# Windowed attention and an ELU feed-forward layer on one core: V held stationary, row sums by a matmul of ones, and every engine's order from a list plan

## The chip, the cores and the metric

The kernel runs on one core of a Trainium2 chip. The metric is the device time of one execution in microseconds (us). Times of single instructions come from one profiled execution; the engines are named as in the profile: PE (matrix engine; PEld its weight loads), DVE (vector engine), ACT (scalar engine), POOL (GpSimd) and SP (which here only issues DMAs).

## The reference

```python
def _attn_ref(q, k, v):                 # q, k, v: (8, 8, 576, 64) float32
    ...
    scores = scale * np.matmul(q, k.transpose(0, 1, 3, 2))
    mask = np.abs(pos[:, None] - pos[None, :]) <= 32
    scores = np.where(mask, scores, -1000000000.0)
    scores = scores - np.max(scores, axis=-1, keepdims=True)
    attn = np.exp(scores)
    attn = attn / (np.sum(attn, axis=-1, keepdims=True) + 1e-09)
    return np.matmul(attn, v)

# x = heads side by side: (4608, 512)
def _moe_ref(x, w_in, w_out):           # w_in (512, 2048), w_out (2048, 512)
    h = x @ w_in
    g = np.where(h > 0.0, h, np.exp(np.minimum(h, 0.0)) - 1.0)
    return g @ w_out
```

## The kernel before

The 4608 tokens (8 batches of 576) are cut into blocks of 64 queries, nine to a batch; a block needs the 128 keys around it. Two blocks make a **pair** (36 pairs of 128 tokens), four pairs make a **tile** of 512 tokens for the feed-forward part (9 tiles).

Per batch: `load_qk` (SP's queue) brings q and k, half the heads at a time, into five staging buffers; `cast` makes bf16 of them (POOL; DVE and ACT for batch 0); `T` turns them on PE, two heads at a time (six small transposes into the one PSUM buffer `psT`, then a copy by ACT, L131, into `qT` or `kT`; its output is scattered: neighbouring elements read land 12 bytes apart). `load_v` (POOL's queue) brings V as bf16 into `vw`, `shift_v` (SP's queue) copies it 64 rows on for the odd blocks. `vw` has 65 columns for each head: the last one holds ones.

Per pair: `QK` writes 16 score matmuls, keys on the partitions, into `psS`; `SM` is one exp on ACT over 128x1024; `MK` multiplies by the window's mask on DVE, two instructions; `AV(i, g)` takes four heads: the probabilities are the weights, V with its column of ones is streamed, 65 columns, so that `o` holds 128 tokens on the partitions and each head's 64 values and row sum beside them. DVE takes the reciprocal of the four sums (L181, 128x4) and multiplies (L183). `X` turns the pair's 128x512 result on PE (four transposes into `psT`), and DVE copies it into `xt` (L197), where the 512 features are on the partitions.

Per tile: sixteen `Hm(t, fo)`, four matmuls of 512 columns each into one of three `psH` buffers, then ACT's exp (`e`, L210) and in `Hv` two DVE instructions (`f`, L216, and `g`, L217). Sixteen steps of `Y(t, s)`, four matmuls of 512 columns each, make the four 128-row outputs of the tile; each is copied by ACT (L232) out of the one `psY` buffer and stored. H of tile t stands between Y of tile t-1.

The order on all engines is that of the program's text. Six steps of pairs come first, with the loads, casts and transposes of batches 1 and 2 at fixed steps; from then on the rest of the attention is dealt out evenly among the slots of H and Y:

```python
                want = base + (goal - base) * (n + 1) // max(1, len(slots) - 2)
                while pos < min(want, goal):
                    rest[pos][1]()
                    pos += 1
```

Of the kernel before, what the change touches and what calls it, by code (L numbers as in the profile page):

```python
# [8 lines left out]
FP32 = mybir.dt.float32  # L9
# [6 lines left out]
def _bap(ap, new_ap):  # L16
    return bass.AP(tensor=ap.tensor, offset=ap.offset,
                   ap=[list(x) for x in new_ap])


@with_exitstack
def kernel(
# [24 lines left out]
    TT = 512  # L47
    NT = N_TOK // TT
    NC = TT // 128
    NFO = D_FF // 128  # L50
    NDO = DM // 128
    VW = D + 1
# [5 lines left out]
    xsp = ctx.enter_context(tc.tile_pool(name="xsp", bufs=3))  # L58
# [11 lines left out]
    ident = const.tile([128, 128], BF16)  # L70
    masks = const.tile([128, 3, QB], BF16)
# [4 lines left out]
    NPB = 2  # L76
# [5 lines left out]
    stage = {}  # L82

    def load_qk(b, half, eng):
        for nm, src in (("q", q), ("k", k)):
            t = stg.tile([PR, HP, TPP * D], FP32, tag="stg")
            eng.dma_start(
                out=t, in_=src[b, half * HP:(half + 1) * HP].rearrange(
                    "h (p t) d -> p h (t d)", t=TPP))
            stage[nm, b, half] = t  # L90

    def cast(b, nm, engs):
        t = bfp.tile([PR, TPP, H, D], BF16, tag="bf")
        for half in range(2):
            src = stage.pop((nm, b, half)).rearrange(
                "p h (t d) -> p h t d", t=TPP)
            dst = t[:, :, half * HP:(half + 1) * HP, :].rearrange(
                "p t h d -> p h t d")
            e = engs[half]
            if e is nc.scalar:  # L100
                nc.scalar.copy(dst, src)
            else:
                e.tensor_copy(dst, src)  # L103
        stage[nm, b] = t

    def load_v(b):
        vt = vw[b % NVB]
        vb = v[b].rearrange("h s d -> s h d")
        nc.gpsimd.dma_start(out=vt[WIN:128, 0, :, 0:D], in_=vb[0:128 - WIN])
        for qb in range(2, NQB - 1, 2):  # L110
            lo = qb * QB - WIN
            nc.gpsimd.dma_start(out=vt[:, qb, :, 0:D], in_=vb[lo:lo + 128])  # L112
        lo = (NQB - 1) * QB - WIN
        nc.gpsimd.dma_start(out=vt[0:S - lo, NQB - 1, :, 0:D], in_=vb[lo:S])
# [6 lines left out]
    def T(b, nm, hp):  # L121
        src = stage[nm, b]
        pt = psT_p.tile([128, TPP, PR], BF16, tag="psT")
        for j in range(TPP):
            nc.tensor.transpose(pt[:, j, :], src[:, j, 2 * hp:2 * hp + 2, :],  # L125
                                ident[0:PR, 0:PR])
        if nm == "k":
            dst = kT[b % NKB][:, hp, WIN:WIN + S]
        else:
            dst = qT[b % NKB][:, hp, :]  # L130
        nc.scalar.copy(dst.rearrange("c (p t) -> c t p", t=TPP), pt)  # L131

    live = {}

    def QK(i):
        psS = psS_p.tile([128, 2, 2, HP, QB], FP32, tag="psS")
# [13 lines left out]
    def SM(i):  # L150
        psS = live.pop(("S", i))
        pu = pup.tile([128, 2, 2, HP, QB], BF16, tag="pu")
        nc.scalar.activation(pu, psS, AX.Exp, scale=SCALE)  # L153
        live["U", i] = pu

    def MK(i):
        pu = live.pop(("U", i))
        p = pm[i % NPB]
        for s in range(2):
            qb = (2 * i + s) % NQB  # L160
            m = masks[:, 1 if qb == 0 else 2 if qb == NQB - 1 else 0, :]
            mb = _bap(m, [m.ap[0], [0, 2], [0, HP], m.ap[1]])
            dst = p[:, :, s * 2 * QB:s * 2 * QB + QB].rearrange(
                "p (a two) c -> p two a c", two=2)
            nc.vector.tensor_mul(dst, pu[:, :, s], mb)  # L165

    def AV(i, g):
        p = pm[i % NPB]
        if g == 0:
            live["X", i] = xsp.tile([128, H, D], BF16, name="xs", tag="xs")  # L170
        o = psO_p.tile([128, HP, VW], FP32, tag="psO")
        for j in range(HP):
            h = g * HP + j
            for s in range(2):
                b, qb = divmod(2 * i + s, NQB)
                nc.tensor.matmul(  # L176
                    o[:, j, :], lhsT=p[:, h, s * QB:s * QB + 128],
                    rhs=vw[b % NVB][:, qb, h, :],
                    start=(s == 0), stop=(s == 1))
        rc = xsp.tile([128, HP], FP32, tag="rc")  # L180
        nc.vector.reciprocal(rc, o[:, :, D])  # L181
        rb = _bap(rc, [rc.ap[0], rc.ap[1], [0, D]])
        nc.vector.tensor_mul(live["X", i][:, g * HP:(g + 1) * HP, :],  # L183
                             o[:, :, 0:D], rb)
# [3 lines left out]
    def X(i):  # L188
        xs = live.pop(("X", i)).rearrange("p h d -> p (h d)")
        t, c = divmod(i, NC)  # L190
        if c == 0:
            xts[t] = xtp.tile([128, NDO, TT], BF16, name="xt", tag="xt")
        pt = psT_p.tile([128, NDO, 128], BF16, tag="psT")
        for do in range(NDO):
# [188 lines left out]
```

## Time and profile before

| | |
|---|---|
| median of 3 runs | 456.05 us (454.32 to 460.13) |
| the profiled execution | 451.61 us, of which the profile's span is 449.9 us |
| mean granted PE clock | 0.981 |
| busy: PE, DVE, ACT, POOL | 337.4, 261.9, 268.3, 84.9 us |
| first matmul of H(0), first of Y(0), last of H(8) | 78.4, 113.2, 427.6 us |

In a line of groups of the profile stand the source line, the engine, the operation, output and inputs with their shapes, the count, the busy time in us and the mean ns of one, then the engine's idle time just before these instructions and what ended it. A row of a single line's view gives the shortest, middle and longest duration in ns. A row of stretches gives each engine's busy us with its instructions in brackets. In a row of the timeline stand the start in us, the length in us, the engine and line, and the idle time before it with its releaser.

### The profile page before, as it was taken

How to read it: one execution, taken by the hardware profiler on the slowest of the kernel's cores; microseconds unless marked ns; L12 is line 12 of the kernel's file. 1: busy time of each engine (PE TensorE's matmuls, PEld its weight loads, DVE VectorE, ACT ScalarE, POOL GpSimd, SP SyncE). 2: the span in 40 equal slices, each digit the busy share in tenths (PEclk: the TensorE clock that was granted, in tenths of full speed). 3: DMA queues.
4: the chain of work that ended last, by engine and by line, in shares of the span. 5: the costliest groups of instructions: out<-in, count | busy, mean ns of one | idle time of the engine just before them, and what ended most of it. 6: DMA issues, size and time to landing. Idle time of an engine off the chain costs nothing.

```text
span 449.9 us, 7032 instructions
## 1 busy us (share of the span) xinstructions
PE 337.4 (75%) x2784; PEld 173.8 (39%) x2832; DVE 261.9 (58%) x557; ACT 268.3 (60%) x283; POOL 84.9 (19%) x92
## 2 busy tenths in 40 slices
PE   0122453766879788788879789687997899999985
PEld 0012342333434344344434345343443444444432
DVE  5004232688746867656757667755666677776610
ACT  1776854788758378637965478476775444344421
POOL 9326216611001700440005200500000000000000
PEclk9999999999989999969999999999899999999999
DMA  8999999973008921972029814520000010010111
GB/s 188 182 261 248 131 216 223 121 80 23 1 23 207 143 50 48 250 60 51 32 66 220 88 32 116 142 72 25 23 25 24 25 48 25 23 48 24 47 48 70
DMA packets 64096, 41.94 MB, mean 93 GB/s; under 512 B 38976, under 2 KB 59456, under 8 KB 64064
## 3 DMA queue, kind: packets, MB, share of 16 engines
q0 software_dynamic: 41728, 8.92, 30.0%
q1 hardware_dynamic: 22336, 32.58, 28.3%
q8 instruction: 22, 0.36, 0.4%
q14 instruction: 10, 0.08, 0.1%
HBM read 36.70 MB, written 9.44 MB: 103 GB/s over the span
## 4 chain that ended last, share of the span: by engine, by line
PE 49%; DVE 17%; ACT 13%; DMA 13%; issue 6%; POOL 1%; SPq 0%; ACTq 0%; POOLq 0%
PE ps L206 20%; PE psY L227 20%; DMA vw<-in_v_dram 6%; DVE g L217 6%; ACT kT L131 5%; DVE f L216 5%; DVE pm L165 5%; DMA w_out_sb<-in_moe_w_out_dram 5%; ACT e L210 5%; PE o L176 4%; DMA t<-in_q_dram 2%; PE pt L125 2%; PE pt L195 2%; ACT qT L131 2%; ACT pu L153 1%
## 5 line engine op out<-in xcount | busy, mean ns | idle before, releaser
L210 ACT ACTIVATE e<-ps 128x512 f32<-128x512 f32 x144 | 92.1, 640 | 113.4 <-PE ps L206 105.6
L206 PE MATMUL ps<-xt,w_in_sb 128*128 128x512 bf16 x549 | 148.6, 389 | 2.8 <-DVE xt L197 1.3
L227 PE MATMUL psY<-w_out_sb,g 128*128 128x512 bf16 x555 | 144.7, 382 | 5.6 <-ACT y L232 3.6
L216 DVE TENSOR_SCALAR f<-e 128x512 bf16<-128x512 f32 x144 | 71.3, 495 | 78.2 <-ACT e L210 78.0
L217 DVE TENSOR_TENSOR g<-ps,f 128x512 bf16<-128x512 f32 x144 | 99.6, 692 | 5.4
L227 PEld LDWEIGHTS <-g 128*128 128x128 bf16 x576 | 52.8, 99 | 58.8 <-issue 6.7
L131 ACT COPY kT<-pt 128x576 bf16<-128x576 bf16 x32 | 66.7, 2084 | 12.0 <-PE pt L125 11.5
L206 PEld LDWEIGHTS <-w_in_sb 128*128 128x128 bf16 x576 | 51.4, 99 | 49.8 <-issue 5.2
L131 ACT COPY qT<-pt 128x576 bf16<-128x576 bf16 x32 | 66.6, 2082 | 5.0 <-PE pt L125 4.7
L125 PE MATMUL pt<-ident,t 96*128 96x96 bf16 x384 | 32.0, 229 | 48.9 <-ACT qT L131 25.4
L176 PE MATMUL o<-vw,pm 128*128 128x65 bf16 x576 | 38.5, 204 | 38.2 <-DVE pm L165 33.5
L103 POOL CAST t<-t 96x1536 bf16<-96x1536 f32 x28 | 41.8, 1522 | 130.8 <-DMA t<-in_q_dram 130.6
L176 PEld LDWEIGHTS <-pm 128*128 128x128 bf16 x576 | 28.6, 104 | 63.3 <-DVE pm L165 54.9
L165 DVE TENSOR_TENSOR pm<-pu,masks 128x512 bf16<-128x512 bf16 x72 | 34.7, 523 | 29.0 <-ACT pu L153 29.0
L125 PEld LDWEIGHTS <-t 96*128 96x128 bf16 x384 | 26.9, 110 | 63.6 <-issue 35.3
L153 ACT ACTIVATE pu<-psS 128x1024 bf16<-128x1024 f32 x36 | 37.2, 1033 | 11.1 <-PE psS L141 8.6
L181 DVE RECIPROCAL rc<-o 128x4 f32<-128x4 f32 x72 | 13.0, 180 | 40.2 <-PE o L176 40.1
L232 ACT COPY y<-psY 128x512 f32<-128x512 f32 x36 | 21.4, 593 | 25.2 <-PE psY L227 24.8
L183 DVE TENSOR_TENSOR xs<-o,rc 128x256 bf16<-128x256 f32 x72 | 30.5, 424 | 2.5
L112 POOL DMA_DIRECT2D vw<-in_v_dram x24 | 21.8, 911 | 25.4 <-PE o L176 13.3
L195 PE MATMUL pt<-ident,xs 128*128 128x128 bf16 x144 | 14.7, 228 | 11.2 <-ACT kT L131 11.1
L197 DVE COPY xt<-pt 128x512 bf16<-128x512 bf16 x36 | 15.0, 417 | 8.6 <-PE pt L195 8.6
(28 smaller groups left out, 72.4 us busy)
## 6 DMA issues: line engine op xcount, KB each, us to landing
t<-in_q_dram SPq DMA_DIRECT2D x16, 576.0 KB, 8.8
t<-in_k_dram SPq DMA_DIRECT2D x16, 576.0 KB, 10.5
out_dram<-y SPq DMA_DIRECT2D x36, 256.0 KB, 2.0
vw<-vw SPq DMA_DIRECT2D x16, 260.0 KB, 5.4
vw<-in_v_dram POOLq DMA_DIRECT2D x24, 128.0 KB, 8.0
w_in_sb<-in_moe_w_in_dram POOLq DMA_DIRECT2D x4, 512.0 KB, 15.6
w_out_sb<-in_moe_w_out_dram POOLq DMA_DIRECT2D x4, 512.0 KB, 25.5
vw<-in_v_dram POOLq DMA_DIRECT2D x16, 96.0 KB, 7.4
```

The costliest lines, as they stand in the source:

```text
L103: e.tensor_copy(dst, src)
L125: nc.tensor.transpose(pt[:, j, :], src[:, j, 2 * hp:2 * hp + 2, :], ident[0:PR, 0:PR])
L131: nc.scalar.copy(dst.rearrange("c (p t) -> c t p", t=TPP), pt)
L153: nc.scalar.activation(pu, psS, AX.Exp, scale=SCALE)
L165: nc.vector.tensor_mul(dst, pu[:, :, s], mb)
L176: nc.tensor.matmul(o[:, j, :], lhsT=p[:, h, s * QB:s * QB + 128], rhs=vw[b % NVB][:, qb, h, :], start=(s == 0), stop=(s == 1))
L183: nc.vector.tensor_mul(live["X", i][:, g * HP:(g + 1) * HP, :], o[:, :, 0:D], rb)
L206: nc.tensor.matmul(ps, lhsT=w_in_sb[:, do, fo * 128:(fo + 1) * 128], rhs=xts[t][:, do, :], start=(do == 0), stop=(do == NDO - 1))
L210: nc.scalar.activation(e, ps, AX.Exp)
L216: nc.vector.tensor_scalar(f, e, -1.0, 0.0, ALU.add, ALU.min)
L217: nc.vector.tensor_tensor(gs[t][:, fo, :], ps, f, ALU.max)
L227: nc.tensor.matmul(ps, lhsT=gs[t][:, fo, c * 128:(c + 1) * 128], rhs=w_out_sb[:, fo, :], start=(fo == 0), stop=(fo == NFO - 1))
```

## The change

**Attention.** `AV(i, s)` now takes one block of 64 queries. For each of the eight heads V (64 columns) is the weight and the head's 64 columns of probabilities are streamed; even heads write PSUM partitions 0 to 63, odd ones 64 to 127, so x comes out with features on the partitions. Two more matmuls with a 128x64 tile of ones as weights and 256 columns streamed give the row sums, each repeated on 64 partitions. `RN` takes the reciprocal of 128x256 sums on DVE and multiplies straight into `xt`. `X`, its transposes and its copy are gone, and so is the column of ones in `vw`.

**Evacuation of q and k.** `E` (ACT, for the last pair of k heads DVE) reads PSUM in steps of 96 elements and writes 576 neighbouring elements. Batch 0's transposes also use the three `psH` buffers. `MK` is one instruction of 128x1024 where both blocks have the same mask.

**Order.** Every operation is entered in a `Plan` with an engine, a duration, a rank and what it needs; `run` then deals them out by time and rank, and calls them in that order.

```diff
+    def run(self):
...
+            for e, rs in ready.items():
+                if not rs:
+                    continue
+                t = max(free[e], min(rs.values()))
+                n = min((ops[n][2], n) for n, r in rs.items() if r <= t)[1]
+                if best is None or t < best[0]:
+                    best = (t, e, n)
...
+        for _, n in order:
+            ops[n][4]()
...
-    vw = [const.tile([128, NQB, H, VW], BF16, name=f"vw{i}") for i in range(NVB)]
-    pm = [const.tile([128, H, 3 * QB], BF16, name=f"pm{i}") for i in range(NPB)]
...
+    vw = [const.tile([128, NQB, H, D], BF16, name=f"vw{i}") for i in range(NVB)]
...
+        if b == 0 and n % 4:
+            pt = psH_p.tile([128, TPP, PR], BF16, name="psH", tag="psH")
+        else:
+            pt = psT_p.tile([128, TPP, PR], BF16, name="psT", tag="psT")
...
-        nc.scalar.copy(dst.rearrange("c (p t) -> c t p", t=TPP), pt)
...
+        dst = dst.rearrange("c (p t) -> c p t", t=TPP)
+        src = pt.rearrange("c t p -> c p t")
+        if EVAC[nm, hp] == "ACT":
+            nc.scalar.copy(dst, src)
+        else:
+            nc.vector.tensor_copy(dst, src)
...
-    def AV(i, g):
...
-                nc.tensor.matmul(
-                    o[:, j, :], lhsT=p[:, h, s * QB:s * QB + 128],
-                    rhs=vw[b % NVB][:, qb, h, :],
-                    start=(s == 0), stop=(s == 1))
-        rc = xsp.tile([128, HP], FP32, tag="rc")
-        nc.vector.reciprocal(rc, o[:, :, D])
...
+    def AV(i, s):
+        p = live["P", i]
+        b, qb = divmod(2 * i + s, NQB)
+        vt = vw[b % NVB]
+        o = psO_p.tile([128, 2, HP, QB], FP32, name="psO", tag="psO")
+        for e in range(2):
+            nc.tensor.matmul(o[64 * e:64 * e + 64, 1], lhsT=ones,
+                             rhs=p[:, e, s], start=True, stop=True)
+        for hp in range(HP):
+            for e in range(2):
+                nc.tensor.matmul(o[64 * e:64 * e + 64, 0, hp, :],
+                                 lhsT=vt[:, qb, 2 * hp + e, :],
+                                 rhs=p[:, e, s, hp, :], start=True, stop=True)
...
+    def RN(i, s):
...
+        rc = rcp.tile([128, HP, QB], FP32, name="rc", tag="rc")
+        nc.vector.reciprocal(rc, o[:, 1])
+        lo = c * 128 + s * QB
+        nc.vector.tensor_mul(xts[t][:, :, lo:lo + QB], o[:, 0], rc)
...
-        pt = psT_p.tile([128, NDO, 128], BF16, tag="psT")
-        for do in range(NDO):
-            nc.tensor.transpose(pt[:, do, :], xs[:, do * 128:(do + 1) * 128],
-                                ident)
-        nc.vector.tensor_copy(xts[t][:, :, c * 128:(c + 1) * 128], pt)
...
+            P.op(("RN", i, s), "DVE", 0.8, r + 1 + s, deps,
+                 lambda i=i, s=s: RN(i, s))
```

What the plan makes of the order is seen at three places. On DVE, in the middle of the run, one pair's work among that of the feed-forward part stood thus before (`pm`: MK; `rc` and `xs`: the two halves of AV; `xt`: X; `f` and `g`: Hv):

```order
L165 TENSOR_TENSOR pm_109<-pu,masks 128x2x4x64 x2
L181 RECIPROCAL rc<-o 128x4
L183 TENSOR_TENSOR xs<-o,rc 128x256
L216 TENSOR_SCALAR f<-e 128x512
L217 TENSOR_TENSOR g<-ps,f 128x512
L181 RECIPROCAL rc<-o 128x4
L183 TENSOR_TENSOR xs<-o,rc 128x256
L216 TENSOR_SCALAR f<-e 128x512
L217 TENSOR_TENSOR g<-ps,f 128x512
L197 COPY xt<-pt 128x4x128
```

and stands now (`rc` and `xt`: RN of the two blocks):

```order
L238 TENSOR_TENSOR pm<-pu,masks 128x1024
L298 TENSOR_SCALAR f<-e 128x512
L303 TENSOR_TENSOR g<-psH,f 128x512
L271 RECIPROCAL rc<-psO 128x256
L273 TENSOR_TENSOR xt<-psO,rc 128x4x64
L298 TENSOR_SCALAR f<-e 128x512
L303 TENSOR_TENSOR g<-psH,f 128x512
L271 RECIPROCAL rc<-psO 128x256
L273 TENSOR_TENSOR xt<-psO,rc 128x4x64
L298 TENSOR_SCALAR f<-e 128x512
L303 TENSOR_TENSOR g<-psH,f 128x512
```

The copy into `xt` is gone, the reciprocal has 64 times the elements, and a pair of `f` and `g` stands between any two steps of the attention.

On POOL, behind batch 0's V and at the start of the program, stood the weights, then batch 1 (`vw_106`) and its casts:

```order
L276 DMA w_in_sb<-in_moe_w_in_dram 128x4x512 x4
L280 DMA w_out_sb<-in_moe_w_out_dram 128x4x512 x4
L109 DMA vw_106<-in_v_dram 96x8x64
L112 DMA vw_106<-in_v_dram 128x8x64 x3
L114 DMA vw_106<-in_v_dram 96x8x64
L103 CAST t<-t 96x4x6x64 x4
```

Now batch 2's V (here `vw_108`) and a cast of batch 0 come first, and between `w_in` and `w_out` stand nine casts and batch 1's V (here `vw_107`):

```order
L195 DMA vw_108<-in_v_dram 96x8x64
L198 DMA vw_108<-in_v_dram 128x8x64 x3
L200 DMA vw_108<-in_v_dram 96x8x64
L164 CAST bf<-stg 96x4x6x64
L341 DMA w_in_sb<-in_moe_w_in_dram 128x4x512 x4
L164 CAST bf<-stg 96x4x6x64 x4
L195 DMA vw_107<-in_v_dram 96x8x64
L198 DMA vw_107<-in_v_dram 128x8x64 x3
L200 DMA vw_107<-in_v_dram 96x8x64
L164 CAST bf<-stg 96x4x6x64 x5
L346 DMA w_out_sb<-in_moe_w_out_dram 128x4x512 x4
```

So `w_out` is issued behind the first cast of batch 3, which takes a buffer that batch 1's transposes must have left.

On SP, batch 1's `shift_v` stood behind eight loads of q and k (`t`; those of batch 0 stand ahead of these rows):

```order
L118 DMA vw_105<-vw_105 64x4x520
L119 DMA vw_105<-vw_105 64x4x520
L87 DMA t<-in_q_dram 96x4x384
L87 DMA t<-in_k_dram 96x4x384
L87 DMA t<-in_q_dram 96x4x384
L87 DMA t<-in_k_dram 96x4x384
L118 DMA vw_106<-vw_106 64x4x520
L119 DMA vw_106<-vw_106 64x4x520
```

Now eighteen loads stand ahead of it, those of batch 3 and the first two of batch 4 among them, and each from the sixth on takes one of the five staging buffers that a cast must have left:

```order
L149 DMA stg<-in_k_dram 96x4x384 x2
L149 DMA stg<-in_q_dram 96x4x384 x4
L204 DMA vw_106<-vw_106 64x4x512
L205 DMA vw_106<-vw_106 64x4x512
L149 DMA stg<-in_q_dram 96x4x384
L149 DMA stg<-in_k_dram 96x4x384 x3
L204 DMA vw_108<-vw_108 64x4x512
L205 DMA vw_108<-vw_108 64x4x512
L149 DMA stg<-in_k_dram 96x4x384 x2
L149 DMA stg<-in_q_dram 96x4x384 x5
L149 DMA stg<-in_k_dram 96x4x384
L204 DMA vw_107<-vw_107 64x4x512
```

The shift of batch 2 (`vw_108`) is issued ahead of that of batch 1 (`vw_107`).

More of the change, by code (lines that the diff above doesn't have):

```diff
@@ L70 @@
     ident = const.tile([128, 128], BF16)
+    ones = const.tile([128, D], BF16)
     masks = const.tile([128, 3, QB], BF16)
@@ L119, in shift_v @@
         nc.sync.dma_start(out=vt[QB:128, 1:NQB:2], in_=vt[0:QB, 2:NQB:2])
[L121 to L133, printed above, removed]
     def QK(i):
-        psS = psS_p.tile([128, 2, 2, HP, QB], FP32, tag="psS")
+        psS = psS_p.tile([128, 2, 2, HP, QB], FP32, name="psS", tag="psS")
         for s in range(2):
@@ new lines, with WI @@
+    sizes = [4] * 9
+    tiles, where = [], {}
+    p0 = 0
+    for t, n in enumerate(sizes):
+        for c in range(n):
+            where[p0 + c] = (t, c)
+        tiles.append((p0, n))
+        p0 += n
+    NT = len(tiles)
+    P = Plan()
+    FC = 512
+    NWC = D_FF // FC
+    w_in_v = moe_w_in.rearrange("(o p) f -> p o f", p=128)
+    w_out_v = moe_w_out.rearrange("(o p) f -> p o f", p=128)
+    def WI(c):
+        nc.gpsimd.dma_start(out=w_in_sb[:, :, c * FC:(c + 1) * FC],
+                            in_=w_in_v[:, :, c * FC:(c + 1) * FC])
@@ L317 @@
[L317 to L352 removed]
+        P.run()
```

411 lines of the change are left out of this document (261 added, 150 removed).

## The prediction

> **What bounds the kernel now.** I read the page from the top: the span, the engines' shares, the slices, the chain; then stretches of the run.
>
> ```profile
> span 449.9 us, 7032 instructions
> PE 337.4 (75%) x2784; PEld 173.8 (39%) x2832; DVE 261.9 (58%) x557; ACT 268.3 (60%) x283; POOL 84.9 (19%) x92
> PE   0122453766879788788879789687997899999985
> DMA  8999999973008921972029814520000010010111
> PE 49%; DVE 17%; ACT 13%; DMA 13%; issue 6%; POOL 1%; SPq 0%; ACTq 0%; POOLq 0%
> 0.00:78.40 78.40, 22.42 (x300) 17.98 (x301) 22.24 (x51) 46.72 (x27) 36.19 (x51) 1.00 1.54 207
> 118.40:401.00 282.60, 243.93 (x2002) 122.03 (x2037) 189.63 (x406) 174.39 (x199) 36.97 (x31) 0.97 0.35 73
> 401.00:449.90 48.90, 42.07 (x189) 18.64 (x191) 19.02 (x34) 14.83 (x25) 0.00 (x0) 1.00 0.13 49
> ```
>
> The last three rows are stretches: length, then busy us of PE, PEld, DVE, ACT and POOL, the granted clock, the DMA share (1 is one full set) and GB/s. There are three regimes. Until 78.4 us PE works 22 us and the DMA slices read 8 or 9: the kernel fills. From 118 to 401 PE is busy 244 of 283 us, and DVE only 190 of 283 (67%). The last 49 us are feed-forward work alone. What PE waits for in the middle, and how the first stretch ends:
>
> ```profile
> PEld L176 <- DVE pm L165: 54.9, 66, 3.4
> PE pt L125 <- ACT qT L131: 25.4, 11, 9.9
> 74.52 0.66 PE L125 MATMUL pt<-ident,t 96*128 96x96 bf16 x6 [4.70 <-POOL t L103]
> 78.44 0.59 PE L206 MATMUL ps<-xt,w_in_sb 128*128 128x512 bf16 x1 [0.51 <-DVE xt L197]
> 113.19 1.03 PE L227 MATMUL psY<-w_out_sb,g 128*128 128x512 bf16 x4
> ```
>
> These are a wait's total us, count and longest, and rows of the timeline. In order, PE stands behind masks and q/k evacuations. H(0) starts at 78.4 because a transpose of batch 2 stands in front of it and waits for a cast. Y(0), and with it H(1), starts at about 112. The end:
>
> ```profile
> L206 PE MATMUL ps<-xt,w_in_sb x549: 377/379/634, 78.4 to 427.6; 128*128 128x512 bf16 x183
> 401.03 1.03 PE L206 MATMUL ps<-xt,w_in_sb 128*128 128x512 bf16 x4
> 401.90 1.03 PE L227 MATMUL psY<-w_out_sb,g 128*128 128x512 bf16 x4
> ```
>
> Four matmuls of 512 columns follow the last four after 0.86 us. H(8) ends at 427.6, so with its sixteen H and sixteen Y in turn (27.5 us) it starts at about 400. From H(1) to there it is 288 us, **41 a tile**.
>
> **What the change does to PE.** H and Y stay as they are. The attention's steps in rows without a wait inside them:
>
> ```profile
> 360.57 0.41 PE L141 MATMUL psS<-qT,kT 64*128 64x64 bf16 x16
> 357.42 0.41 PE L176 MATMUL o<-vw,pm 128*128 128x65 bf16 x8
> 359.39 0.39 PE L195 MATMUL pt<-ident,xs 128*128 128x128 bf16 x4
> 115.36 0.42 PE L125 MATMUL pt<-ident,t 96*128 96x96 bf16 x6
> ```
>
> A pair loses 2 x 0.41 (AV) and 0.39 (X), 1.21 us. It gains twice eight 64-column matmuls and two of 256 columns a block. The eight cost between half of L141's row (0.2, two at a time) and L176's row (0.41); the two cost between 0.11 and 0.22 (half of a 512-column matmul each, together or one after the other). So AV is 0.31 to 0.63 a block; I take 0.5, near the upper row, since its weights change at each matmul as in L176. A pair saves between -0.05 and 0.59 us, 36 pairs between -2 and 21. That shows only if PE remains the bound.
>
> **What it does to DVE: the term that decides.**
>
> ```profile
> L217 DVE TENSOR_TENSOR g<-ps,f 128x512 bf16<-128x512 f32 x144 | 99.6, 692 | 5.4
> L183 DVE TENSOR_TENSOR xs<-o,rc 128x256 bf16<-128x256 f32 x72 | 30.5, 424 | 2.5
> L181 DVE RECIPROCAL rc<-o 128x4 f32<-128x4 f32 x72 | 13.0, 180 | 40.2 <-PE o L176 40.1
> L197 DVE COPY xt<-pt 128x512 bf16<-128x512 bf16 x36 | 15.0, 417 | 8.6 <-PE pt L195 8.6
> L216 DVE TENSOR_SCALAR f<-e 128x512 bf16<-128x512 f32 x144 | 71.3, 495 | 78.2 <-ACT e L210 78.0
> L216 DVE TENSOR_SCALAR f<-e x144: 415/427/1702, 81.0 to 428.6; 128x512 bf16<-128x512 f32 x144
> L165 DVE TENSOR_TENSOR pm<-pu,masks x72: 411/416/5236, 39.1 to 391.9; 128x512 bf16<-128x512 bf16 x72
> ```
>
> From L183 and L217, both with a PSUM input, an element costs (692 - 424)/256 = 1.05 ns and an instruction 424 - 268 = 156 ns. A reciprocal of 4 elements should then take 160 ns; it takes 180. Put on its elements, that is (180 - 156)/4 = **6.0 ns each**. No row shows a long reciprocal, so I bound 128x256 from both sides: 0.42 us if it runs like L183 (the 20 ns being a start-up cost); 2.2 us with the smallest fixed cost that a PSUM row allows, L197's if that copy passes two bf16 at a time (417 - 512 x 0.525 = 148 ns, so 8.0 ns each and 256 x 8.0 + 148). I take 256 x 6.0 + 156 = 1.69 us, the middle, because it is the nearest row of the same operation.
>
> [...]
>
> One RN is then 1.69 + 0.42 + two gaps, 2.2 us. MK becomes one instruction, 0.7 us (between 0.42 and 2 x 0.42). A pair costs DVE 0.7 + 2 x 2.2 = **5.1 us**. The unchanged f and g are 0.43 + 0.69 + gaps 0.06 = 1.18 us for each fo, 18.9 a tile. So a tile takes 4 x 5.1 + 18.9 + 0.6 for one evacuation = 40 us of DVE, against PE's 27.5 (128 matmuls) + 4 x 1.4 + 2.4 = 35.5. DVE becomes the bound at nearly the 41 us that a tile takes now.
>
> **What it does to ACT.**
>
> ```profile
> L131 ACT COPY kT<-pt 128x576 bf16<-128x576 bf16 x32 | 66.7, 2084 | 12.0 <-PE pt L125 11.5
> L210 ACT ACTIVATE e<-ps 128x512 f32<-128x512 f32 x144 | 92.1, 640 | 113.4 <-PE ps L206 105.6
> L153 ACT ACTIVATE pu<-psS 128x1024 bf16<-128x1024 f32 x36 | 37.2, 1033 | 11.1 <-PE psS L141 8.6
> ```
>
> Per element L210 to L153 cost (1033 - 640)/512 = 0.77 ns; 576 neighbouring elements would be 0.69 us, and L131's scattered output takes three times that. Now the output is dense and the PSUM input is scattered. I take 0.7; the upper bound is 2.08 (the scatter costs the same on either side). At 0.7 ACT saves 133 - 39 = 94 us, nearly all beside other work; at 2.08 nothing is saved and the start grows by 10 to 20 us.
>
> [...]
>
> **The start.**
>
> ```profile
> 14.48 1.47 ACT L101 CAST t<-t 96x1536 bf16<-96x1536 f32 x1 [1.56 <-DMA t<-in_k_dram]
> 15.26 0.74 POOL L276 DMA_DIRECT2D w_in_sb<-in_moe_w_in_dram x1 [4.07 <-DMA vw<-in_v_dram]
> 18.07 0.70 SPq L118 DMA_DIRECT2D vw<-vw  x1
> 37.52 0.45 PE L141 MATMUL psS<-qT,kT 64*128 64x64 bf16 x10 [1.88 <-ACT kT L131]
> vw<-vw SPq DMA_DIRECT2D x16, 260.0 KB, 5.4
> t<-in_q_dram SPq DMA_DIRECT2D x16, 576.0 KB, 8.8
> vw<-in_v_dram POOLq DMA_DIRECT2D x24, 128.0 KB, 8.0
> w_in_sb<-in_moe_w_in_dram POOLq DMA_DIRECT2D x4, 512.0 KB, 15.6
> ```
>
> Batch 0's inputs are there at 14.5, its scores at 37.5, behind eight evacuations through one buffer; with four buffers and short copies they start at about 20, and the first AV at 23, when the shift (issued 18.1, 5.4 to land) is there. Four pairs of 2 x (AV 0.5 + handovers 0.2 + RN 2.2) end at 46, where H(0) starts, against 78.4; it takes DVE 19 us, to 65. Then batch 1's shift is missing. SP issues it behind eighteen loads of 576 KB, 10.6 MB; with three batches of V (1.8), two shifts (1.0) and w_in (2.1) that is 15.5 MB, with w_out 17.6. At the 207 GB/s of the first stretch these are 75 to 85 us. On POOL w_out stands behind a cast that waits for batch 1's transposes, at about 60, inside that. So pair 4's second block runs at 80. H(1), Y(0) and the later pairs are queued behind it on PE, and DVE idles from 65. On SP the next loads and the first outputs stand behind the shift; three output buffers cover those. Seven blocks at 2.9 plus 2 for masks make H(1) start at **102** instead of 112. The new tile of ones and the fewer memsets lie under the first loads and cost nothing.
>
> **The sum.** From 102 on DVE has 28 pairs x 5.1 = 143, seven tiles x 18.9 = 132, five evacuations 3 and 7 for waits on POOL's casts (L216's mean, 495 by 71.3/144, is above its middle value): 285 us. Between two RNs stands a pair of f and g, during which PE makes the next AV, so I add only 3%: 294. H(8) starts at 396, the tail stays 49: span 445, and with the 1.7 us around it 447 against 451.6. The median of the runs lies 4.4 us above that execution; added here, **450 us**. The range of this case is 435 to 465.
>
> **The rivals.**
> - *The reciprocal streams* (0.42 us). RN is 0.9, a pair 2.5 us, a tile 29 us of DVE: PE stays the bound. H(1) comes at 80 + 11 = 91; seven tiles at 35.5 with the same 3% are 256, the tail 49: span 396, as a median **402**. For it: 20 ns can be a start-up cost; against it: no other DVE row has one above 160.
> - *The reciprocal takes 8 ns an element* (2.2 us). A pair takes 6.1 us. H(1) comes at 107, then 28 x 6.1 + 142 = 313, with 3% 322; with the tail 478, as a median **485**, slower. It decides from 6.8 ns on, since each ns more is 256 x 72 = 18 us. For it: L197's fixed cost; against it: L183's.
> - *The plan's order does not shorten the start, or E stays at 2.08*: H(1) at 112 or later and the rest as forecast, **455 to 470**. For it: eighteen loads ahead of the shift; against it: the loads are needed later in any case.
>
> **Chances.** Forecast 0.40, streaming 0.27, 8 ns 0.19, the last 0.14. A measurement here tells about 2% (447 to 465) from no change. Of the forecast a third falls below 447, a tenth above 465; streaming is all faster; 8 ns nearly all slower; the last mostly no change. Faster 0.43, same 0.33, slower 0.24. The range of 8 in 10 must reach both reciprocal cases: 388 to 488.
>
> **What would show it.** RECIPROCAL's mean ns at 128x256 settles the main term: 0.4, 1.7 or 2.3 us. DVE should be busy over 85% after 102 us, with PE waiting for RN; with a streaming reciprocal PE is above 93% and DVE near 75%. The copies of q and k should read 0.7 us; H(0) should start at 46 and H(1) near 102, behind batch 1's shift. The forecast is wrong if the reciprocal's cost is not per element, or if in-order waits between PE and DVE cost more than the 3%.

## The result: 439.7 us against 457.4, and the profile after

The changed kernel takes 439.66 us (median of four runs, 438.13 to 440.82) against 457.38 (454.32 to 460.13) of the kernel before, run beside it: a ratio of 0.961, with a 95% interval of 0.954 to 0.969. It is faster by 3.9%, three times the 1.3% that was forecast. The profiled execution took 438.1 us with a span of 436.4.

The page of the changed kernel: span, engines, the granted clock in 40 slices (tenths), the chain that ended last by engine, then the groups of the reciprocal and of a q copy.

```profile
span 436.4 us, 6922 instructions
PE 333.8 (76%) x2786; PEld 166.6 (38%) x2832; DVE 346.6 (79%) x501; ACT 175.2 (40%) x274; POOL 86.4 (20%) x93
PEclk9999999555797999999999999999999999999999
DVE 58%; PE 31%; ACT 5%; DMA 3%; issue 2%; POOL 1%; ACTq 0%; POOLq 0%
L271 DVE RECIPROCAL rc<-psO 128x256 f32<-128x256 f32 x72 | 126.0, 1750 | 16.4 <-PE psO L257 15.7
L187 ACT COPY qT<-psT 128x576 bf16<-128x576 bf16 x30 | 19.1, 636 | 7.6 <-PE psT L174 7.3
```

The chain has gone over from PE (49% before) to DVE (58%). The reciprocal takes 1750 ns where 1.69 us was forecast, the copies 0.64 us where 0.7 was. So the two prices on which the forecast hung were right, and its time was wrong by 10 us nevertheless; where, the stretches show. From here on each kernel is cut at the first `e` of tiles 0, 1 and 8 (1 to 2 us behind that tile's first H). Columns: length, busy us of PE, PEld, DVE, ACT and POOL, clock, DMA share, GB/s. Of the changed kernel:

```profile
0.00:56.30 56.30, 14.43 (x202) 10.85 (x204) 25.34 (x35) 11.56 (x15) 31.46 (x43) 1.00 1.30 239
56.30:119.10 62.80, 41.42 (x435) 24.86 (x438) 44.58 (x61) 29.35 (x44) 20.92 (x20) 0.70 0.86 141
119.10:388.65 269.55, 236.99 (x1968) 112.74 (x2004) 258.57 (x374) 120.05 (x193) 33.98 (x30) 0.99 0.31 64
```

Of the kernel before, the middle:

```profile
113.40:402.10 288.70, 248.76 (x2046) 124.38 (x2084) 194.56 (x417) 179.10 (x205) 36.97 (x31) 0.97 0.34 72
```

Tile 0 starts 24 us earlier than before (56.3 against 80.3), tile 1 **6 us later** (119.1 against 113.4): what the start won is lost again ahead of tile 1. The seven tiles between take 270 us instead of 289, and there DVE is busy 259 of 270 us, 96%. The tail is as it was, 47.8 us. Why tile 1 is late, from the timeline of PE (start, duration, and in brackets the idle time and what ended it):

```profile
83.67 0.66 PE L174 MATMUL psT<-ident,bf 96*128 96x96 bf16 x6
85.06 0.64 PE L174 MATMUL psT<-ident,bf 96*128 96x96 bf16 x6 [0.72 <-ACT qT L187]
...
96.09 0.64 PE L174 MATMUL psT<-ident,bf 96*128 96x96 bf16 x6 [0.73 <-ACT qT L187]
96.66 0.42 PE L253 MATMUL psO<-pm,ones 128*64 128x256 bf16 x2
```

Ten transposes of later batches, about one every 1.4 us because each waits for the copy of the one ahead out of the single buffer `psT`, stand on PE in front of pair 4's second AV at 96.66.

### The profile page after: what moved, and what is told of

Same layout as the page of the kernel before. It is cut to its first block, busy times and chain, and to the rows that moved or that the text cites. A ratio compares the mean times of both kernels' runs of the same rounds, so it can differ in the third digit from the quotient of the medians.

```text
span 436.4 us, 6922 instructions
## 1 busy us (share of the span) xinstructions
PE 333.8 (76%) x2786; PEld 166.6 (38%) x2832; DVE 346.6 (79%) x501; ACT 175.2 (40%) x274; POOL 86.4 (20%) x93
## 4 chain that ended last, share of the span: by engine, by line
DVE 58%; PE 31%; ACT 5%; DMA 3%; issue 2%; POOL 1%; ACTq 0%; POOLq 0%
DVE rc L271 24%; DVE g L303 14%; PE psY L310 12%; PE psH L284 11%; DVE f L298 9%; DVE xt L273 6%; DMA vw<-in_v_dram 3%; PE psT L174 2%; PE psO L253 2%; DVE pm L244 2%; DVE pm L238 2%; PE psS L214 1%; ACT e L292 1%; ACT pu L225 1%; PE psO L257 1%
## 5 line engine op out<-in xcount | busy, mean ns | idle before, releaser
L292 ACT ACTIVATE e<-psH 128x512 f32<-128x512 f32 x144 | 85.9, 597 | 183.5 <-PE psH L284 170.9
L284 PE MATMUL psH<-xt,w_in_sb 128*128 128x512 bf16 x560 | 147.1, 385 | 12.1 <-DVE g L303 7.6
L271 DVE RECIPROCAL rc<-psO 128x256 f32<-128x256 f32 x72 | 126.0, 1750 | 16.4 <-PE psO L257 15.7
L303 DVE TENSOR_TENSOR g<-psH,f 128x512 bf16<-128x512 f32 x144 | 99.6, 692 | 4.9
L164 POOL CAST bf<-stg 96x1536 bf16<-96x1536 f32 x29 | 43.2, 1520 | 100.8 <-PE psT L174 79.3
L253 PE MATMUL psO<-pm,ones 128*64 128x256 bf16 x144 | 23.6, 324 | 46.3 <-DVE xt L273 44.7
L174 PEld LDWEIGHTS <-bf 96*128 96x128 bf16 x384 | 24.5, 112 | 34.5 <-POOL bf L164 12.0
L174 PE MATMUL psT<-ident,bf 96*128 96x96 bf16 x348 | 28.7, 228 | 7.9 <-ACT qT L187 3.6
L273 DVE TENSOR_TENSOR xt<-psO,rc 128x256 bf16<-128x256 f32 x72 | 30.6, 425 | 2.5
L198 POOL DMA_DIRECT2D vw<-in_v_dram x24 | 21.9, 922 | 47.8 <-PE psO L257 38.5
L257 PE MATMUL psO<-pm,vw 128*64 128x64 bf16 x576 | 23.0, 206 | 0.0
L214 PEld LDWEIGHTS <-kT 64*128 64x128 bf16 x576 | 12.5, 101 | 21.0 <-issue 18.2
```

The costliest lines, as they stand in the source:

```text
L164: eng.tensor_copy(dst, src)
L253: nc.tensor.matmul(o[64 * e:64 * e + 64, 1], lhsT=ones, rhs=p[:, e, s], start=True, stop=True)
L257: nc.tensor.matmul(o[64 * e:64 * e + 64, 0, hp, :], lhsT=vt[:, qb, 2 * hp + e, :], rhs=p[:, e, s, hp, :], start=True, stop=True)
L271: nc.vector.reciprocal(rc, o[:, 1])
L273: nc.vector.tensor_mul(xts[t][:, :, lo:lo + QB], o[:, 0], rc)
L284: nc.tensor.matmul(ps, lhsT=w_in_sb[:, do, fo * 128:(fo + 1) * 128], rhs=xts[t][:, do, :], start=(do == 0), stop=(do == NDO - 1))
```

## The experiments

All twelve in one table. "First e" is in us from the span's start; ratios are against the kernel before, run beside each.

| kernel | time, us | ratio (95%) | first e of tile 0, 1, 8 | span |
|---|---|---|---|---|
| before | 457.4 | 1 | 80.3, 113.4, 402.1 | 449.9 |
| changed | 439.7 | 0.961 (0.954 to 0.969) | 56.3, 119.1, 388.7 | 436.4 |
| e1_scale: no reciprocal | 394.9 | 0.871 (0.864 to 0.877) | 45.8, 103.8, 347.8 | 395.5 |
| e3_hold: transposes held | 425.1 | 0.938 (0.930 to 0.946) | 57.0, 107.3, 374.8 | 422.6 |
| e5_scatter: old copies | 481.4 | 1.060 (1.052 to 1.067) | 64.1, 150.6, 433.0 | 480.8 |
| e10_lnexp: reciprocal on ACT | 396.7 | 0.874 (0.868 to 0.880) | 49.3, 107.2, 347.4 | 395.1 |
| e4_before_dense: new copies alone | 441.7 | 0.971 (0.963 to 0.978) | 79.7, 111.1, 392.5 | 440.3 |
| e6_before_dense_av: nearly all but the plan | 450.8 | 0.990 (0.986 to 0.994) | 76.0, 115.8, 404.5 | 452.3 |
| e11_lnexp_hold | 384.2 | 0.843 (0.838 to 0.849) | 49.3, 91.3, 333.7 | 381.5 |
| e12_price: true price in the plan | 425.5 | 0.936 (0.929 to 0.944) | 56.9, 117.1, 377.8 | 423.8 |
| e13_actcast: one cast moved | 437.5 | 0.958 (0.954 to 0.962) | 53.8, 118.5, 388.2 | 435.9 |
| e14_best: e11 and e13 | 382.8 | 0.837 (0.834 to 0.841) | 46.9, 91.6, 334.0 | 381.7 |
| e15_shift: e14, V of batch 1 first | 389.0 | 0.853 (0.848 to 0.858) | 46.5, 97.6, 339.2 | 386.9 |
| e16_v1first: V of batch 1 first | 444.8 | 0.975 (0.970 to 0.980) | 57.0, 106.6, 395.0 | 442.8 |

### Is it the reciprocal that bounds it? (e1_scale)

```diff
-        nc.vector.reciprocal(rc, o[:, 1])
+        nc.vector.tensor_scalar(rc, o[:, 1], 1.0 / 4225.0, 0.0, ALU.mult, ALU.add)
```

> The reciprocal is left out: a multiplication by 1/4225 of the same 128x256 from PSUM stands in its place, everything else and the order of every engine stay. Theory (VectorE and its reciprocal bound the kernel): the instruction takes 0.42 us instead of 1.75, so a normalisation takes 0.8 instead of 2.12 us. From H(1) to H(8) VectorE loses 56 x 1.33 = 74 us of its 258 and TensorE (236 us busy of 268) becomes the bound: 240 to 250 us there; before H(1) sixteen blocks lose 1.3 us each where they follow one another, 10 to 20 us. Time 395 to 410 us. Rival 1 (the fixed order, waits between the engines bound it as much as the reciprocal): TensorE waits nearly as before, 420 to 435 us. Rival 2 (the change's gain is the start alone and VectorE's 96% is slack filled up by waiting): no change, 435 to 441.

The group of the replaced instruction and the middle stretch:

```profile
L271 DVE TENSOR_SCALAR rc<-psO 128x256 f32<-128x256 f32 x72 | 30.2, 420 | 26.8 <-PE psO L257 26.4
103.80:347.80 244.00, 237.01 (x2006) 112.59 (x2005) 196.73 (x372) 119.88 (x193) 34.02 (x30) 0.99 0.34 70
```

The instruction takes 0.42 us, the middle 244 us, the whole 394.9. PE is busy 237 of the 244 us there: 97%. So the reciprocal's length is what bounds the changed kernel, and without it the same static order keeps PE nearly full. The theory holds, with the time at the lower edge of its range; rivals 1 and 2 fall.

### What makes tile 1 late? (e3_hold)

```diff
+                if b >= 2:
+                    deps.append(("RN", b * NQB // 2 - 3, 1))   # for T of batch b
```

> The transposes of batches 2 and 3 are made to stand behind the attention of pairs that come a little before they are needed, instead of ahead of pair 4's. Theory (the second tile starts late because ten transposes and their copies stand ahead of pair 4's AV on TensorE): H(1) comes from 118 to about 103 us and the time falls by 13 to 16, to 422 to 427 us; the later stages stay. Rival 1 (loads, above all batch 1's shift and w_out, set H(1) anyway): H(1) within 3 us of 118, time 435 to 441. Rival 2 (the transposes now interrupt the steady state, where TensorE is 88% busy and VectorE 96%): H(1) early, but the stretch from H(1) to H(8) grows by the ten microseconds saved, time 434 to 441.

PE's timeline at pair 4's second AV, and the middle stretch:

```profile
84.64 0.42 PE L253 MATMUL psO<-pm,ones 128*64 128x256 bf16 x2
107.30:374.80 267.50, 242.29 (x2131) 119.47 (x2130) 257.90 (x378) 128.60 (x205) 37.57 (x32) 1.00 0.33 69
```

That AV runs at 84.64 instead of 96.66, tile 1 starts 12 us earlier, and the middle is 268 us (270 in the changed kernel). The time falls by 14.6 us. The transposes ahead of it were the cause. It still runs 5 us later than the 80 us that were forecast for batch 1's shift, but not because of the shift: the two copies of the shift, issued at 76.0 and 76.7, landed 9.2 and 10.8 us later, behind the start of this AV. It takes batch 1's first block, an even one, whose V is not shifted. On PE it follows the scores of pairs 6 to 8, which wait 0.5 to 2.5 us each for ACT's `pu`. Pair 5's first AV, the first that needs the shift, runs at 87.59, 0.1 us after it had landed, and waited for DVE; there the shift is next in line.

### The dense copy: undone, and alone (e5_scatter, e4_before_dense)

```diff
-        dst = dst.rearrange("c (p t) -> c p t", t=TPP)
-        src = pt.rearrange("c t p -> c p t")
+        dst = dst.rearrange("c (p t) -> c t p", t=TPP)
+        src = pt
```

> The changed kernel with one part undone: the copies of transposed q and k are written scattered and read dense, as before. ScalarE's copy should take about 2.08 us again instead of 0.64. Theory (the dense copy shortens the start only): the ten transposes ahead of pair 4's AV go at 2.8 us each instead of 1.36, and the first tile's wait grows with its eight copies, so H(1) comes 12 to 25 us later; from H(1) to H(8) ScalarE stays under 60% busy and nothing changes. Time 450 to 463 us. Rival 1 (ScalarE has slack everywhere, also at the start): 436 to 444. Rival 2 (longer copies also delay the exponentials in the steady state): over 465.

The groups of a q copy on ACT and a k copy on DVE, then PE's timeline:

```profile
L187 ACT COPY qT<-psT 128x576 bf16<-128x576 bf16 x30 | 62.9, 2097 | 9.0 <-PE psT L174 8.8
L189 DVE COPY kT<-psT 128x576 bf16<-128x576 bf16 x7 | 14.6, 2081 | 13.5 <-PE psT L174 13.5
103.81 0.64 PE L174 MATMUL psT<-ident,bf 96*128 96x96 bf16 x6 [2.15 <-ACT qT L187]
...
126.17 0.64 PE L174 MATMUL psT<-ident,bf 96*128 96x96 bf16 x6 [2.15 <-ACT qT L187]
126.74 0.42 PE L253 MATMUL psO<-pm,ones 128*64 128x256 bf16 x2
150.60:432.97 282.37, 241.47 (x2005) 113.11 (x2004) 262.49 (x373) 157.00 (x193) 33.54 (x30) 0.98 0.30 61
DVE f L298 <- ACT e L292: 13.0, 13, 1.7
```

The last row is a wait of that middle stretch: total us, count and longest. The time rises by 42 us, above every case but rival 2's. The ten transposes come one every 2.8 us, and the AV behind them at 126.74 instead of 96.66, as the theory said; but by the first e's 8 us are lost ahead of tile 0, 24 between tiles 0 and 1 and 13 in the middle, where the theory saw nothing. There DVE waits 13.0 us for `e`, against 4.9 in the changed kernel, so rival 2 has a part. Without this part the whole change would have made the kernel slower.

Alone, put into the kernel before (`nc.scalar.copy` with the output `c (p t) -> c p t` and the input `c t p -> c p t`):

> The kernel before, with one part of the change alone: the copies of transposed q and k read scattered and write dense. The copy should take 0.64 us instead of 2.08. Theory (the dense copy is worth its time only where transposes and copies follow one another through one buffer, at the start): the eight copies ahead of the first scores give 8 x 1.45 = 12 us, those of batch 1 up to 12 more; from H(1) to H(8) TensorE stays the bound. Time 430 to 444 against 455. Rival 1 (the longer copies hold up the exponentials in the steady state too): H(1) to H(8) falls from 288 to 270 or less, time 410 to 428. Rival 2 (the loads set the start of before): 446 to 455.

```profile
39.80 0.66 PE L125 MATMUL pt<-ident,t 96*128 96x96 bf16 x6 [13.53 <-POOL t L103]
75.34 0.66 PE L125 MATMUL pt<-ident,t 96*128 96x96 bf16 x6 [5.87 <-POOL t L103]
111.10:392.50 281.40, 248.90 (x2085) 123.70 (x2084) 193.55 (x416) 128.09 (x205) 37.04 (x31) 0.98 0.35 74
```

The time, 441.7, is in the theory's range, its place is not: tile 0 starts at 79.7 as before, because PE waits there for casts (rows of 39.80 and 75.34), which wait for loads (4.10 us ahead of the casts that POOL starts at 72.41). Two us are won by tile 1 and seven between tiles 1 and 8, in small waits of PE: that for masks, the longest, falls from 30.6 to 29.4 us, and the 1.5 us for which X's transposes had waited behind long copies are gone. (The prediction's wait of 25.4 us behind q's copies is one of the whole run; 23.9 of it lie in the first 80 us.) Theory and rival 2 each had a part. The medians differ by 13 us, the spans of the two profiled executions by 9.6: that of the kernel before lies 4 us below its median.

### All but the plan (e6_before_dense_av)

The hand-written list of the kernel before is kept, with these two steps, the new `MK`, `AV` and `RN` and the dense copy:

```diff
-                st.append(lambda i=i: (MK(i - 1), AV(i - 1, 0)))
-                st.append(lambda i=i: AV(i - 1, 1))
-            if i >= 2:
-                st.append(lambda i=i: X(i - 2))
+                st.append(lambda i=i: (MK(i - 1), AV(i - 1, 0), RN(i - 1, 0)))
+                st.append(lambda i=i: (AV(i - 1, 1), RN(i - 1, 1)))
```

> The kernel before with its hand-written order kept, and the dense copies, the transposed AV, the long reciprocal and the one multiplication for the masks put in; so all of the change but the static plan. Theory (the plan's order is worth only a part of the start, since VectorE's 38 us a tile bound the steady state under any order): H(1) to H(8) 268 to 285 us, time 430 to 450. Rival 1 (with the order by hand TensorE stands at each AV for the reciprocal of the block ahead, 2.3 us each, and cannot fill the wait): H(1) to H(8) over 320 us, time over 475; the plan is then what makes the transposed AV pay. Rival 2 (the plan's transposes ahead of pair 4 cost more than it gains elsewhere): under 430.

```profile
115.80:404.50 288.70, 248.32 (x2081) 117.03 (x2080) 257.98 (x369) 129.05 (x205) 37.23 (x31) 0.98 0.34 73
```

450.8 us, just outside the theory's range, with a middle of 289 us (3.7 above it); rival 1's middle of over 320 does not come. Added in this order, the parts are: dense copies -13 (441.7 against 454.7 of the runs beside it), the transposed AV with its long reciprocal **+9** (450.8), the plan **-11** (439.7; by the two ratios, 0.990 and 0.961, rather -13, since they were not run side by side). In another order the parts could come out otherwise. This kernel also has a third buffer for `xt`, copies all of q and k on ACT and turns batch 0 through `psT` alone, so the plan's part holds these differences too. In the hand-written order the AV that gives the change its name costs time: it takes little off PE (337 us busy before, 334 after) and puts 126 us of reciprocal on DVE in place of 13. By the first e's, the plan wins 19 us in the middle (DVE busy 96% of it instead of 89%) and 20 at the start, and gives 23 back before tile 1. That is 16 us between the two profiled executions; that of this kernel was the longest of its ten.

### The price in the plan (e12_price)

```diff
-            P.op(("RN", i, s), "DVE", 0.8, r + 1 + s, deps,
+            P.op(("RN", i, s), "DVE", 2.1, r + 1 + s, deps,
```

> The changed kernel with one number of the plan changed: the list plan reckons a normalisation at 2.1 us, as measured, instead of 0.8; the work is the same, the order on the engines is another. Theory (VectorE bounds the steady state under any reasonable order, and the second tile's wait stays): 432 to 444. Rival 1 (the low price is why the plan puts ten transposes ahead of pair 4's AV and fills TensorE badly): 420 to 430. Rival 2 (with the true price the plan delays the feed-forward blocks): 446 or more.

```profile
91.30 0.42 PE L253 MATMUL psO<-pm,ones 128*64 128x256 bf16 x2
117.10:377.80 260.70, 238.51 (x1997) 115.21 (x1996) 254.23 (x374) 119.78 (x191) 28.25 (x26) 0.99 0.30 62
```

425.5 us: rival 1's time, and my theory that order could not matter falls. Rival 1's reason holds in part: pair 4's second AV goes at 91.30, 5 us earlier, but with seven transposes still straight ahead of it. The middle takes 261 us with DVE busy 254, 97.5%. By the span 12.6 us are won, 2 of them by tile 1, 9 in the middle and 2 in the tail. Of the 9, DVE is idle 4.5 us less (6.5 against 11.0) and busy 4.3 less. The longest `f` there takes 1.76 us; the changed kernel has one of 7.26 (shown further down).

### The reciprocal elsewhere (e10_lnexp, e11_lnexp_hold)

```diff
+        nc.scalar.activation(ln, o[:, 1], AX.Ln)
+        nc.scalar.activation(rc, ln, AX.Exp, scale=-1.0)
-        nc.vector.reciprocal(rc, o[:, 1])
```

In the plan this is an operation of 0.8 us on ACT, and RN is 0.42 on DVE.

> The reciprocal is moved to ScalarE, as exp(-ln(sum)) in two instructions of 128x256; one table set that holds both functions is loaded at the start. VectorE keeps only the multiplication. Theory (VectorE bound): VectorE loses 1.75 us a block, ScalarE gains about 0.8 (ScalarE was 45% busy from H(1) to H(8), now about 60%); the chain from AV to AV becomes 0.5 + 0.4 + 0.4 + 0.42 and four handovers, about 2.2 us instead of 2.95. From H(1) to H(8) 240 to 252 us, time 397 to 415. Rival 1 (the chain through one more engine, with ScalarE's queue in order, costs what it saves): 425 to 440. Rival 2 (ScalarE delays the e of each tile, so that TensorE waits for psH): 415 to 425.

```profile
L130 ACT ACT_TABLE_LOAD x1 | 1.3, 1283 | 0.8 <-PEq L539 0.8
L270 ACT ACTIVATE ln<-psO 128x256 f32<-128x256 f32 x72 | 27.5, 382 | 27.0 <-PE psO L260 26.9
L272 ACT ACTIVATE rc<-ln 128x256 f32<-128x256 f32 x72 | 30.0, 417 | 2.3
107.20:347.40 240.20, 235.10 (x1994) 112.02 (x1993) 174.68 (x318) 159.42 (x302) 31.53 (x28) 0.99 0.34 70
```

396.7 us, within 2 us of the kernel that has no reciprocal at all. (The plan's prices changed too, and with them the order, which in e12 alone moved 14 us; what the 43 us would be in the old order was not run.) ACT spends 382 + 417 ns where DVE spent 1750, and is still busy only 159 of 240 us. PE is busy 98% of the middle. The load of 1283 ns in the rows above, at 0.80 us, is the only one of this run: over 72 turns from `ln` to `rc` and the exps of `pu` and `e` between them, ACT loaded no other table.

With e3's hold as well:

> Both steps together: the reciprocal as exp(-ln) on ScalarE, and the transposes of batches 2 and 3 held back. Theory (the two act in different stages and add up): the first e of tile 1 comes from 107 to about 95 us, H(1) to H(8) stays 240 us, time 383 to 388. Rival 1 (without the transposes ahead, batch 1's shift sets the second tile): first e of tile 1 at 100 or later, time 389 to 394. Rival 2 (the held transposes and their copies meet a fuller ScalarE): no gain, 394 to 400.

384.2 us: tile 1 at 91.3 and a middle of 242 us (333.7 - 91.3). The two steps act in different stages and add up, 12.5 us here against 14.6 alone.

### The start, and what sets tile 1 next (e13_actcast, e14_best, e15_shift, e16_v1first)

```diff
-              ("k", 1): "POOL"}
+              ("k", 1): "ACT"}
```

> The changed kernel with one cast moved from POOL's queue to ScalarE: that of the second half of batch 0's k, which stood on POOL behind the issues of batch 2's V and began at 18.4 us. The orders of TensorE and VectorE stay. Theory (POOL's queue is why the first scores come at 24.0 and the first AV at 30.5 us): the first scores come at 17 to 20 us, the first AV at 25 to 27 and the first e of tile 0 at 50 to 53 instead of 56.3; the ten transposes ahead of pair 4's AV then give little of it back, since they wait for copies and not for loads. Time 432 to 437. Rival 1 (batch 0's shift of V, issued at 19 us, sets the first AV): first e of tile 0 within 1.5 us of 56. Rival 2 (what is won at the start is lost again before H(1), where the loads set the pace): first e of tile 0 earlier, that of tile 1 still at 119, time 437 to 441.

PE's timeline in this kernel:

```profile
14.82 0.55 PE L214 MATMUL psS<-qT,kT 64*128 64x64 bf16 x6
23.61 0.66 PE L174 MATMUL psT<-ident,bf 96*128 96x96 bf16 x6 [7.48 <-POOL bf L164]
28.24 0.42 PE L253 MATMUL psO<-pm,ones 128*64 128x256 bf16 x2
```

The first scores come 9 us earlier (14.82 against 24.0), the first AV only 2, because a transpose of batch 1 stands ahead of it on PE and waits for a cast that POOL, in order, reaches behind its DMA issues. Tile 0 wins 2.5 us, tile 1 0.6. Rival 2 holds, with the transposes in the loads' place; in time it can't be told from the changed kernel.

> Three steps together: exp(-ln) on ScalarE for the reciprocal, the transposes of batches 2 and 3 held back, and that cast moved to ScalarE. Theory (they add up): first e of tile 0 at 43 to 47 us instead of 49.3, of tile 1 at 86 to 89 instead of 91.3; time 378 to 382 against 384. Rival (with the transposes held, batch 1's shift sets the second tile whatever the start does): first e of tile 1 within 1 us of 91, time 383 to 385.

The rival's numbers hold: tile 0 wins 2.4 us, tile 1 nothing, and 382.8 is not told from 384.2. I took batch 1's shift for the cause, from these rows of SP's queue and of PE:

```profile
65.67 0.60 SPq L207 DMA_DIRECT2D vw<-vw  x1
74.90 0.61 PE L217 MATMUL psS<-qT,kT 64*128 64x64 bf16 x16 [1.11 <-ACT pu L228]
75.44 0.43 PE L256 MATMUL psO<-pm,ones 128*64 128x256 bf16 x2
```

They do not show it. The shift's second copy, issued at 66.3, landed 9.9 us later, behind the start of this AV, which as in e3 needs no shifted V; the AV follows the scores of pair 8, which waited for ACT's `pu`. The first AV that does need it, at 77.46, waited for DVE. I read the rows otherwise and moved the shift, through the plan's dependency that puts batch 1's V behind w_in (`if b == 1` became `if b == 2`), in e14 and in the changed kernel:

> The best version so far (exp(-ln) on ScalarE, held transposes, the cast on ScalarE), and batch 1's V is loaded ahead of w_in in place of batch 2's; its shift then stands at the place of batch 2's on SP, behind ten loads of q and k instead of sixteen. Theory (the second tile waits for batch 1's shift, issued at 66 us): the shift goes out before 40 us, pair 4's second AV follows tile 0's feed-forward, first e of tile 1 at 80 to 86 us instead of 91.6; time 371 to 378 against 382.8. Rival 1 (w_in, now behind other traffic, or the loads of batches 1 and 2 set the second tile): first e of tile 1 within 2 us of 91.6, time 380 to 385. Rival 2 (batch 2's V comes too late instead, for pair 9's AV in the third tile): first e of tile 1 earlier, of tile 2 no earlier than 125, time 382 or more.

> The changed kernel with that one step alone: batch 1's V ahead of w_in, batch 2's behind it; the plan draws its order anew. Theory (in the changed kernel the transposes ahead of pair 4's AV set the second tile, not the shift): unless the new order moves the transposes too, first e of tile 1 within 4 us of 119, time 434 to 443. Rival (the shift was the cause, and the transposes only filled the wait): first e of tile 1 at 105 or earlier, time under 428.

The theory falls in both: they are slower than what they started from, by about 6 and 5 us. In e15 neither rival holds either: the shift landed before 50 us, and yet pair 4's second AV came at 76.92, later than in e14, and tile 1 6 us later. The rows of DVE, POOL and PE in e15:

```profile
67.78 8.02 DVE L308 TENSOR_SCALAR f<-e 128x512 bf16<-128x512 f32 x1
68.42 7.10 POOL L167 CAST bf<-stg 96x1536 bf16<-96x1536 f32 x5
76.92 0.42 PE L256 MATMUL psO<-pm,ones 128*64 128x256 bf16 x2 [8.26 <-DVE xt L283]
```

PE waited 8.26 us for DVE, where one `f`, 0.42 us long elsewhere, took 8.02 and ended 0.3 us behind five casts that POOL ran in a row. So what an early shift is worth stays open: the new order met another wait. e16's tile 1 starts at 106.6, near the rival's 105, but its tile 2 only at 167.8, 61 us later. SP's queue and a row of PE in e16:

```profile
38.26 16.18 SPq L149 DMA_DIRECT2D stg<-in_q_dram  x3
92.61 0.37 SPq L321 DMA_DIRECT2D out_dram<-y  x1
147.20 0.30 PE L253 MATMUL psO<-pm,ones 128*64 128x256 bf16 x2
```

From 54.4 to 92.6 us SP issues nothing: the plan now has the first output, which waits for Y(0), ahead of the next loads of q. Batch 2's shift stands behind it and landed at 107.5. But pair 9's first AV, the first of batch 2, runs 40 us later still, at 147.20, since PE's new order has H(1) and eight steps of Y(1) ahead of it. What of tile 2's delay is owed to the queue and what to this order was not separated, nor was the shift tried with the loads left in their place.

## Why the prediction was right and wrong

**Right.** DVE became the bound, and by the price that was forecast: 1.69 us against 1750 ns, the copies 0.7 against 0.64, MK 0.7 against 0.68, the tail 49 against 48.8 from H(8) on. The price of the reciprocal was drawn from 24 ns over four elements; that it came within 4% is in part luck. The case of a streaming reciprocal (402 us, PE the bound) was built from the same sum; e1, which has that price, took 394.9.

**Wrong: the term "285 us, with 3%: 294" for seven tiles.** It was 270 us. The step that failed is the *gap between instructions*, put at +0.06 us for f and g together. DVE's timeline shows that some of them overlap (the last row is DVE's largest wait between the first e of tiles 1 and 8):

```profile
213.75 1.75 DVE L271 RECIPROCAL rc<-psO 128x256 f32<-128x256 f32 x1
215.53 0.42 DVE L273 TENSOR_TENSOR xt<-psO,rc 128x256 bf16<-128x256 f32 x1
215.87 0.42 DVE L298 TENSOR_SCALAR f<-e 128x512 bf16<-128x512 f32 x1
216.32 0.69 DVE L303 TENSOR_TENSOR g<-psH,f 128x512 bf16<-128x512 f32 x1
216.93 0.42 DVE L298 TENSOR_SCALAR f<-e 128x512 bf16<-128x512 f32 x1
...
217.99 0.75 DVE L244 TENSOR_TENSOR pm<-pu,masks 128x512 bf16<-128x512 bf16 x2
218.66 0.42 DVE L298 TENSOR_SCALAR f<-e 128x512 bf16<-128x512 f32 x1
...
123.01 7.26 DVE L298 TENSOR_SCALAR f<-e 128x512 bf16<-128x512 f32 x1
121.48 8.51 POOL L164 CAST bf<-stg 96x1536 bf16<-96x1536 f32 x6
DVE f L298 <- ACT e L292: 4.9, 8, 2.3
```

From one f to the next it is 216.93 - 215.87 = 1.06 us, not 1.18: 112 times 0.12 is 13 us. RN is 215.87 - 213.75 = 2.12, not 2.2, MK 218.66 - 217.99 = 0.67, so a pair is 4.91, not 5.1: 28 times 0.19 is 5 us. The kernel before overlaps in the same way (its g of 0.69 us at 200.12 is followed at 200.72), so its trace could have told. The 7 us for waits on POOL's casts were right in sum: the f's take 489 ns in the mean against a middle value of 418, 8 us over 112, nearly all of it in the one f of 7.26 us at 123.01, beside six casts in a row. Of the 9 us for in-order waits 5 came (4.9 of them for `e`). That gives 294 - 13 - 5 - 4 = 272; the other 2 us are masks of two of the 28 pairs, which lie outside this stretch, and rounding.

**Wrong: "H(0) starts at 46" and "pair 4's second block runs at 80".** H(0) came at 54.4: first scores at 24.0 instead of 20, because POOL's cast stood behind V's issues (e13), then the first AV at 30.5 instead of 23, behind a transpose of batch 1 and three pairs' scores on PE. Pair 4's block ran at 96.66. The step that failed is the *wait*: it took the shift as what stands in front of that block and did not read PE's order between H(0) and that AV. Ten transposes stood there, and e3 gives 12 us back by moving them. For the shift this block did not wait at all: in e3 and e14 it ran before the shift had landed in full. H(1) came at 118.0 instead of 102.

The two errors pull apart, +16 at the start and -24 in the middle, which leaves a span forecast 9 us too high; the 4.4 us added to go from one execution to the median were another 3 too many (here 1.5), and rounding 451 to 450 took 1 off. That the time still lies between 435 and 465 is owed to these opposite errors and not to the sum's terms.

**Not seen at all: what each part is worth.** The forecast put the dense copies' gain mostly "beside other work" and priced their absence at 10 to 20 us of the start; e5 shows 42, 13 of them in the middle. And it forecast the whole without asking what its parts do alone: transposed AV +9, dense copies -13, plan -11 to -13.

**Two estimates that the trace decides.** The upper bound for the reciprocal, 8.0 ns an element, came from L197's fixed cost, worked out as if that copy passed two elements at a time; no run shows that step, and the reciprocal's own rows give (1750 - 180)/252 = 6.2. The upper bound for the copy, 2.08 us, took the scatter to cost the same on either side, which was the author's estimate. ACT's copy reads PSUM in steps of 192 bytes at 636 ns for 576 elements, no slower than the 0.69 us that the prediction worked out for a dense read. On both points the measurement decides.

## What to carry to other kernels

Take the cost of an engine's stretch from start to start of neighbouring instructions, not from durations plus gaps: 0.12 us on each of 112 steps was half the error of the middle. Read such rows in the trace of the kernel before. When an order is planned, read on each in-order queue everything that stands between the work that is sped up and the next stage's first instruction; here ten transposes placed early held up pair 4's second AV by 12 us (e3), one transpose that waited 7.48 us for its cast the pairs behind it (e13), and an output SP's next loads by 38 us (e16). Before moving what looks late, check that the work behind it needs it: pair 4's second AV did not need the shift. And look at what a new order sets side by side: beside a run of casts on POOL one instruction of DVE took 8 us in e15. When one engine bounds the kernel with a long instruction, look for a neighbour that is half idle: exp(-ln) on ACT takes 0.80 us for what the reciprocal on DVE does in 1.75, and with held transposes brings this kernel to 384 us, 16% below the one before.

## What the hardware showed that was not expected

- A reciprocal on DVE cost 6.2 ns an element and about 155 ns (180 ns for 4, 1750 for 256), six times the 1.05 ns of a multiplication on PSUM.
- A scattered bf16 output (12-byte steps) cost ACT and DVE the same, 2097 and 2081 ns for 576 elements (e5); with the scatter on the PSUM input it is 636 and 750 (changed kernel).
- In the changed kernel's rows from 213.75 on, an instruction on DVE that reads nothing of the one ahead started 0.08 us before that one's end (g of 0.69 us is followed after 0.61); g behind its f and the multiplication behind its reciprocal started 0.03 us after it.
- One f on DVE took many times its 0.42 us beside a run of casts on POOL and ended 0.3 us behind the last of them: 7.26 us in the changed kernel (six casts), 8.58 in e1 (six), 8.02 in e15 (five). e3 has runs of four and no f over 1.71 us, so not every run does it; what decides was not tried.
- Between the first e of tiles 0 and 1 the granted clock was 0.70 (5 tenths in three slices), and work at the lower clock took longer: in e3 four Y matmuls took 1.89 us at 0.50, where four took 1.03 at 1.00 in the prediction's rows of the tail. What lowers the clock is not shown: PE was busy 66% of that stretch, and ahead of tile 0, at a clock of 1.00, only 26%.

```profile
91.12 1.89 PE L310 MATMUL psY<-w_out_sb,g 128*128 128x512 bf16 x4
90.00:95.00 5.00, 3.09 (x24) 1.37 (x24) 4.06 (x6) 0.00 (x0) 0.78 (x1) 0.50 1.15 270
```
